# Folding w_phi into the key weights with two row tiles of 64 rows

## The chip, the cores and the metric

The kernel runs on one core of one Trainium2 chip. The metric is the device time of one execution in microseconds (us); lower is better. A core has five engines that run their own instruction streams: TensorE (PE; its weight loads are shown apart as PEld), VectorE (DVE), ScalarE (ACT), GpSimd (POOL) and SyncE (SP), which here issues the DMAs. Matrix products go from SBUF to PSUM, from which ScalarE or VectorE reads them.

## The reference

Two identical layers are applied to x (2048 tokens, D = 640). Each layer has a linear attention and a dense part; the attention has 32 heads of 20 columns:

```python
qkv = layernorm(x) @ wqkv                        # q, k, v, per head 20 columns
pq, pk = q @ w_phi, k @ w_phi                    # per head, 20 x 20
phi = concat(softmax(p), softmax(-p))            # 40 features per head
kv, z = phi_k^T v, sum(phi_k)
x = x + (phi_q kv / (phi_q z + 1e-6)) @ wo
x = x + mish(layernorm(x) @ w1 + b1) @ w2
```

## The kernel before

**Folding.** A softmax does not change when one number is taken from all its inputs, so the kernel subtracts the last of the 20 columns of each head from the other 19 and keeps 19 columns per head. It multiplies w_phi, shifted in this way, into the query and key weights once, at the start of the first layer. The result is a matrix of 640 rows (five chunks k of 128) and 32 x 19 = 608 columns. It is kept in two parts, a rounded high part (`r1h`, written by ScalarE out of PSUM) and the rest (`r1l`, written by VectorE as PSUM minus the high part); every later product uses high times high, high times low and low times high.

`load_raw` fetches the transposed query or key weights in six tiles (`raw`), 120 rows (six heads) each for the first four and 80 rows (four heads) for the last two. `bd` holds w_phi as block diagonals of 120 x 120, `shift_phi` does the subtraction on GpSimd. `fold_part` (L258) multiplies one `raw` tile, 128 columns of it at a time as the stationary operand, with one block of `bd`. For a chunk, three such products fill 18 heads (342 columns) in one PSUM bank and three more the other 14 heads (266 columns) in another, and `fold_end` (L286) evicts each bank by one ScalarE and one VectorE instruction. `fold_phi` (L290) does this for the keys in two visits within the first block of tokens: four half chunks in two `mm` tiles (two PSUM banks each), and later six half chunks in two `mm` tiles and two `one` tiles (a bank each). There are two `mm` buffers and four `one` buffers, which all projections share.

**Projections and features.** The 2048 tokens are worked through in eight blocks of two tiles of 128. `project` computes a tile of keys, queries or values by 30 matmuls (L414). `features` makes the softmax pairs: copy out of PSUM on ScalarE, maximum and minimum on VectorE (L439), two subtractions (L440 and L442), the exponential on ScalarE, sums and reciprocals on VectorE (L448, L449), and the scaling on GpSimd (L450). Subtraction L440 is on GpSimd for queries and on VectorE for keys, as the argument `pool_sub` says. Then query features are transposed on VectorE (L505) and written to DRAM (`e_d`), and key features are multiplied with the values into `kva` (L491). In the second half of the layer `average` (L768) uses column halves: outputs of 64 partitions, each with its own stationary operand of 64 columns.

**Order.** The start of the first layer stands in a `written()` block, in which instructions stay in the order of the text. Behind it a planner orders the instructions of each engine by simulated times; `tc.issue_after` keeps an instruction behind another one. Within an engine the order is fixed when the program is built. The DMAs of SP are spread over eight completion counters in turn, and each waits until the DMA eight places earlier has landed. In the first block the order of the work is q0, v0, first visit of the fold, v1, second visit, k0, q1, k1; the statistics of block 1 (L307, L309, L319) and its normalization (`xn`, L135) lie in between on VectorE, GpSimd and ScalarE.

Of the kernel before, what the change touches and what calls it, by code (L numbers as in the profile page):

```python
# [8 lines left out]
F32 = mybir.dt.float32  # L9
# [7 lines left out]
P = 128  # L17
# [27 lines left out]
def kernel(  # L45
# [22 lines left out]
    def mm_tile():  # L68
        return psum.tile([P, 2, 512], F32, tag="mm", name="mm", bufs=2)

    def one_tile():
        return psum.tile([P, 512], F32, tag="one", name="one", bufs=4)
# [169 lines left out]
    def load_raw(which, ts=range(6)):  # L242

        raw = []
        for t in ts:
            rows = 120 if t < 4 else 80
            if t < 5:
                r = wts.tile([P, D], F32, tag=f"r2{'hl'[which]}{5 + t}", name=f"raw{which}{t}")
            else:
                r = r2_wide(10 + which, F32)[:, 0]  # L250

            n = P if t < 5 else rows
            c0 = which * D + (t * 120 if t < 5 else D - rows)
            nc.sync.dma_start(r[:n], wqk_t[c0:c0 + n, :])
            raw.append((r, rows))
        return raw

    def fold_part(ps, k, t, bd, raw):  # L258

        r, rows = raw[t]  # L260
        heads = rows // DH
        n = DL * (6 * (t % 3) if t < 5 else 10)
        ins = nc.tensor.matmul(ps[:, n:n + heads * DL].rearrange("p (j d) -> p j d", d=DL), r[:rows, k * P:(k + 1) * P],
                         bd[:rows, t, :rows].rearrange("p (j d) -> p j d", d=DH)[:, :, :DL], start=True, stop=True)
        last_product[0] = ins.ins
# [20 lines left out]
    def fold_end(ws, ps, k, c):  # L286
        fold_high(ws, ps, k, c)
        fold_low(ws, ps, k, c)

    def fold_phi(ws, bd, raw, parts):  # L290

        for n in range(0, len(parts), 2):
            mm = mm_tile() if n < 4 else None
            pair = list(zip(parts[n:n + 2], [one_tile(), one_tile()] if mm is None else [mm[:, 0], mm[:, 1]]))
            with tc.issue_after(last_product[0]):
                for (k, c), ps in pair:
                    for t in range(3 * c, 3 * c + 3):
                        fold_part(ps, k, t, bd, raw)
            for (k, c), ps in pair:
                fold_end(ws, ps, k, c)  # L300


    def norm_stats(t, xt):

# [155 lines left out]
    def attend_first(layer, x_src, first):  # L460
# [18 lines left out]

        def keys(xts, i, v):  # L480
            e = big_tile()
            yield from features(project(xts, i % BT, kv_ws, 0, w=QC), e, False,
                                nc.vector if i == NT - 1 else nc.gpsimd)
            yield
            if i % BT == 0 and BT < i < NT - BT:
                yield
            for r in range(9):
                for j in range(4):
                    h = 3 * (4 * (r // 3) + j) + r % 3
                    if h < H:  # L490
                        nc.tensor.matmul(kva[32 * j:32 * j + DH + 1, 40 * r:40 * r + 40],  # L491
                                         v[:, (DH + 1) * h:(DH + 1) * (h + 1)], e[:, 40 * h:40 * h + 40],
                                         start=(i == 0 and r == 0), stop=(i == NT - 1), skip_group_check=True)
# [32 lines left out]
        if first is None:  # L526
            with written():
                xt = fetch(x_src, 0)
                bd = big_tile()[:120, :720].rearrange("p (t c) -> p t c", t=6)
                nc.sync.dma_start(bd[:, :3], phi_bd[:, :3])  # L530
                raw_q = load_raw(0, range(3))

                nc.vector.memset(bd[:80, 5, :80], 0.0)
                nc.sync.dma_start(bd[:40, 5, :40], phi_bd[80:120, 4, 80:120])
                nc.sync.dma_start(bd[40:80, 5, 40:80], phi_bd[:40, 5, :40])
                nc.sync.dma_start(bd[:, 3:5], phi_bd[:, 3:5])
                shift_phi(bd, slice(0, 3))
                raw_q += load_raw(0, range(3, 6))
                kv_ws = [r1_pair(k) for k in range(KD)]
                raw_v = [fetch_v(k) for k in range(KD)]  # L540
                raw = load_raw(1)
                early = fetch(x_src, 1)
                mvs = [norm_stats(t, xt) for t in range(BT)]
                norm_scale(0, mvs)
                shift_phi(bd, slice(3, 5))
                shift_phi(bd, 5)

                q_ws = [r2_pair(k) for k in range(KD)]
                mm = [mm_tile(), mm_tile()]
                pcs = [one_tile(), mm[0][:, 0], mm[0][:, 1], mm[1][:, 0], mm[1][:, 1]]  # L550
                for t in range(3):
                    for k in range(KD):
                        fold_part(pcs[k], k, t, bd, raw_q)
                xn = [row_tile() for _ in range(BT)]
                act(xn[0], xt[:, 0, :], AF.Identity, bias=stats[:, 0, 1, 0:1], scale=stats[:, 0, 0, 0:1])
                nc.vector.tensor_scalar(xn[1], xt[:, 1, :], stats[:, 0, 0, 1:2], stats[:, 0, 1, 1:2],
                                        op0=ALU.mult, op1=ALU.add)

                def highs(c, ks):
                    for k in ks:  # L560
                        fold_high(q_ws, pcs[k], k, c)

                def lows(c, ks):
                    for k in ks:
                        fold_low(q_ws, pcs[k], k, c)

                def make_v(k, low):
                    split(kv_ws[k][0][:, D:2 * D], kv_ws[k][1][:, D:2 * D], raw_v[k], low)

                def half(c, ks):  # L570
                    project_half(q0[c], nxt, 0, q_ws, 0, c, ks, w=QC)

                highs(0, (0, 1, 2))
                lows(0, (0,))
                nxt = Transposed(xn)
                nxt.turn(one_tile())
                nxt.high()
                lows(0, (1, 2))
                nxt.lower()
                highs(0, (3, 4))  # L580
                pcs[0], pcs[1] = one_tile(), one_tile()
                for k in (0, 1):
                    fold_part(pcs[k], k, 3, bd, raw_q)
                nxt.turn(one_tile())
                for t in (4, 5):
                    for k in (0, 1):
                        fold_part(pcs[k], k, t, bd, raw_q)
                last = mm_tile()
                nxt.turn(last[:, 0])
                nxt.high()  # L590
                nxt.high()
                lows(0, (3, 4))
                nxt.lower()
                nxt.lower()
                highs(1, (0, 1))
                q0 = [one_tile()]
                half(0, (0, 1))
                mm = mm_tile()
                pcs[2], pcs[3] = mm[:, 0], mm[:, 1]
                for k in (2, 3):  # L600
                    for t in range(3, 6):
                        fold_part(pcs[k], k, t, bd, raw_q)
                lows(1, (0, 1))
                half(0, (2, 3))
                make_v(0, nc.gpsimd)
                highs(1, (2, 3))
                lows(1, (2, 3))
                pcs[4] = last[:, 1]
                for t in range(3, 6):
                    fold_part(pcs[4], 4, t, bd, raw_q)  # L610
                half(0, (4,))
                make_v(1, nc.gpsimd)
                highs(1, (4,))
                lows(1, (4,))
                q0.append(one_tile())
                half(1, range(KD))
                for k in (2, 3, 4):
                    make_v(k, nc.vector)
            nc.sync.dma_start(mask, bass.AP(tensor=head_mask.tensor, offset=head_mask.offset,
                                            ap=[[1, 120], [120 * (DH + 1), 3]]))  # L620
        else:
            nxt, kv_ws, turn = first
            with tc.issue_after(last_load[0]):
                load_k_weights(kv_ws)
            q_ws = load_q_weights()
        for b in range(NB):
# [15 lines left out]
            for n, (kind, t) in enumerate(order):  # L642
                t = int(t)
                i = b * BT + t
                if b == 0 and layer == 0 and n in (2, 3):
                    if n == 2:
                        advance()
                    fold_phi(kv_ws, bd, raw, ((0, 0), (1, 0), (2, 0), (3, 0)) if n == 2 else
                             ((4, 0), (0, 1), (1, 1), (2, 1), (3, 1), (4, 1)))
                if b == 0 and n == (1 if layer else 3):  # L650
                    kva = one_tile()
                    nc.vector.memset(kva[:, :360], 0.0)
# [464 lines left out]
```

## Time and profile before

| what | value |
|---|---|
| median of 3 runs | 1357.27 us (1356.24 to 1361.53) |
| the profiled execution | 1357.15 us, its span 1355.4 us |
| PE busy | 1347.9 us, 99% |
| VectorE, ScalarE, GpSimd busy | 78%, 42%, 34% |
| share of PE in the chain that ended last | 94% |

The span is the time from the first to the last instruction. A row of a timeline is: start in us, duration in us (of a merged group from its first start to its last end), engine, line, operation, what it writes `<-` what it reads, shapes, count; in brackets the idle time of the engine before it and what ended that. `raw` and `bd` appear as `raw` and `big` (the buffer that holds `bd`). A row of a table of windows is: the stretch, its length, then for PE, PEld, DVE, ACT and POOL the busy time and number of instructions, the granted TensorE clock, the share of the DMA engines and the rate in GB/s. A row of the chain is: start, duration, engine or DMA, tile, line and count. One f32 matmul is two records of the trace.

### The profile page before, as it was taken

To read this page: it belongs to the slowest core of one execution; us is meant where nothing else is said; L and a number is where in the kernel's file an instruction comes from. 1 tells how busy PE (TensorE), PEld (TensorE's weight loads), DVE (VectorE), ACT (ScalarE), POOL (GpSimd) and SP (SyncE) were. 2 spreads that over 40 slices of the span, in tenths; PEclk is the share of its full clock that TensorE was granted. 3 is DMA by queue.
4 is the path that set the end of the run, shared out by engine and by line. 5 is a ranking of instruction groups with operands and counts; after the bars stand their busy time and mean duration, and the time that the engine had idled before them with its cause. 6 is when DMAs were issued, how large, how long until landed. Compare 5 with 4: busy or idle time off the path is not lost.

```text
span 1355.4 us, 30982 instructions
## 1 busy us (share of the span) xinstructions
PE 1347.9 (99%) x12896; PEld 1337.4 (99%) x12896; DVE 1061.2 (78%) x1799; ACT 575.7 (42%) x968; POOL 462.4 (34%) x417
## 2 busy tenths in 40 slices
PE   9999999999999999999999999999999999999999
PEld 9999999999999999999999999999999999999998
DVE  6888988886787887778769788788768776676775
ACT  5444444212454545445443334332236444444443
POOL 3355544334222222222225655634251211111112
PEclk9999999999999999999999999999999999999999
DMA  9544444698714442244474534548974221233200
GB/s 332 166 101 92 95 111 99 173 289 280 216 35 95 117 118 71 61 104 104 140 231 100 122 79 90 95 102 263 282 259 127 79 68 41 88 98 98 70 29 20
DMA packets 352629, 174.11 MB, mean 128 GB/s; under 512 B 287449, under 2 KB 324041, under 8 KB 352489
## 3 DMA queue, kind: packets, MB, share of 16 engines
q1 hardware_dynamic: 352489, 172.14, 46.9%
q8 instruction: 101, 1.65, 0.5%
q14 instruction: 39, 0.32, 0.1%
HBM read 106.23 MB, written 65.86 MB: 127 GB/s over the span
## 4 chain that ended last, share of the span: by engine, by line
PE 94%; DVE 2%; DMA 2%; POOL 1%; SPq 1%; ACT 0%; issue 0%; POOLq 0%; ACTq 0%
PE mm L414 26%; PE one L892 25%; PE mm L943 24%; PE one L414 12%; PE mm L768 2%; PE one L334 2%; PE one L491 1%; PE one L943 1%; DMA xt<-in_x 1%; PE one L768 1%; DVE r L448 1%; DMA raw<-in_wqk_t 0%; DVE m L439 0%; DMA v<-in_wv 0%; DVE r L442 0%; SPq L508 0%
## 5 line engine op out<-in xcount | busy, mean ns | idle before, releaser
L943 PE MATMUL mm<-r2h,ol 128*128 128x320 f32 x1240 | 296.1, 309 | 0.0
L918 POOL TENSOR_TENSOR ol<-big,ol 128x512 fp32r<-128x512 f32 (+1 forms) x98 | 131.1, 1338 | 477.7 <-ACT ol L917 419.5
L892 PE MATMUL one<-xtl,r1h 128*128 128x256 f32 x960 | 268.2, 279 | 0.0
L892 PE MATMUL one<-xth,r1l 128*128 128x256 f32 x960 | 268.0, 279 | 0.0
L892 PE MATMUL one<-xth,r1h 128*128 128x256 f32 x960 | 265.9, 279 | 0.0
L943 PEld LDWEIGHTS mm<-r2h,ol 128*128 128x128 f32 x1240 | 212.5, 188 | 0.0
L943 PE MATMUL mm<-r2l,ol 128*128 128x320 f32 x620 | 191.2, 309 | 0.0
L414 PE MATMUL mm<-r1h,xth 128*128 128x304 f32 (+1 forms) x600 | 185.2, 309 | 0.0
L414 PE MATMUL mm<-r1l,xth 128*128 128x304 f32 (+1 forms) x600 | 183.7, 306 | 0.0
L414 PE MATMUL mm<-r1h,xtl 128*128 128x304 f32 (+1 forms) x600 | 183.6, 306 | 0.2 <-POOL xtl L351 0.2
L892 PEld LDWEIGHTS one<-xtl,r1h 128*128 128x128 f32 x960 | 180.4, 188 | 0.0
L892 PEld LDWEIGHTS one<-xth,r1l 128*128 128x128 f32 x960 | 180.4, 188 | 0.0
L892 PEld LDWEIGHTS one<-xth,r1h 128*128 128x128 f32 x960 | 179.6, 188 | 0.0
L907 DVE TENSOR_SCALAR big<-big 128x512 f32<-128x512 f32 (+1 forms) x98 | 57.2, 583 | 110.0 <-ACT big L905 109.8
L909 ACT ACTIVATE big<-big,two 128x512 f32<-128x512 f32 (+1 forms) x98 | 70.1, 715 | 116.1 <-DVE big L908 116.1
L917 ACT ACTIVATE ol<-big 128x512 fp32r<-128x512 f32 (+1 forms) x98 | 60.9, 622 | 137.6 <-DVE big L916 137.4
L905 ACT ACTIVATE big<-one,b1s 128x256 f32<-128x256 f32 x192 | 80.9, 468 | 89.0 <-PE one L892 88.5
L450 POOL TENSOR_TENSOR r<-r,r 128x1280 f32<-128x1280 f32 x32 | 77.2, 2413 | 118.9 <-DVE r L449 100.8
L943 PEld LDWEIGHTS mm<-r2l,ol 128*128 128x128 f32 x620 | 116.4, 188 | 0.0
L414 PEld LDWEIGHTS mm<-r1h,xth 128*128 128x128 f32 x600 | 112.8, 188 | 0.9
L414 PEld LDWEIGHTS mm<-r1h,xtl 128*128 128x128 f32 x600 | 112.8, 188 | 0.4 <-POOL xtl L351 0.4
L414 PEld LDWEIGHTS mm<-r1l,xth 128*128 128x128 f32 x600 | 112.8, 188 | 0.1
(161 smaller groups left out, 3142.7 us busy)
## 6 DMA issues: line engine op xcount, KB each, us to landing
e_d<-r SPq DMA_DIRECT2D x128, 160.0 KB, 4.2
big<-e_d SPq DMA_DIRECT2D x32, 640.0 KB, 8.0
x_d<-xt SPq DMA_DIRECT2D x23, 640.0 KB, 4.8
xt<-x_d SPq DMA_DIRECT2D x22, 640.0 KB, 5.3
n_d<-xn SPq DMA_DIRECT2D x168, 80.0 KB, 2.3
xt<-in_x SPq DMA_DIRECT2D x16, 640.0 KB, 4.4
xn<-x_d SPq DMA_DIRECT2D x28, 320.0 KB, 4.4
v<-n_d SPq DMA_DIRECT2D x30, 256.0 KB, 3.0
```

The lines of the kernel that those rows point to most:

```text
L334: nc.tensor.transpose(ps[:, c, t * P:(t + 1) * P], self.rows[t][:, (c0 + c) * P:(c0 + c + 1) * P], ident)
L414: last_product[0] = nc.tensor.matmul(ps[:, :w], a[:, sl], r, start=(k == 0 and n == 0), stop=(k == KD - 1 and n == 2)).ins
L448: nc.vector.tensor_reduce(r, eg, axis=AX.X, op=ALU.add)
L450: ins = scale.tensor_tensor(eg, eg, r.unsqueeze(2).to_broadcast([P, 2 * H, DH]), op=ALU.mult).ins
L768: nc.tensor.matmul(po[c][64 * q:64 * q + 64, GW * j:GW * j + w], phs[g][:n, s0:s0 + 64], kvb[:n, g, :w], start=True, stop=True)
L892: nc.tensor.matmul(ph[:, j, :], l, r, start=(n == 0), stop=(n == 3 * KD - 1))
L905: exps[0] = nc.scalar.activation(part(ta, 0)[:, j - js.start], ph[:, j, :], AF.Exp, bias=b1s[:, 2 * pr + j:2 * pr + j + 1]).ins
L907: nc.vector.tensor_scalar_min(e, e, E_CAP)
L909: nc.scalar.activation(r, n, AF.Ln, bias=two)
L917: nc.scalar.activation(ah[:, js], n, AF.Copy)
L918: nc.gpsimd.tensor_tensor(al[:, js], n, ah[:, js].bitcast(F32), op=ALU.subtract)
L943: ins = nc.tensor.matmul(pys[t][c][:, :HC], (ah, ah, al)[n][:, j, t * P:(t + 1) * P], w, start=(f == 0 and n == 0), stop=(f == KF - 1 and ...
```

## The change

The key weights are folded by another arrangement; the query weights are folded as before.

- `load_phi_halves` builds `ph`, a second copy of w_phi: 64 rows for the first three heads of a `raw` tile and 60 rows for the other three, each with blocks of 60 columns. It is cleared on VectorE, filled by three DMAs ahead of those of the key `raw` tiles, and shifted by one more `shift_phi` on GpSimd.
- The key `raw` tiles are loaded four rows earlier, so that one head triple lies in rows 4 to 63 and the other in rows 64 to 123. The sixth tile has 64 rows instead of 80, of which the last 40 (two heads) count.
- `fold_keys` replaces `fold_phi`. For a chunk it issues 11 matmuls: for each of five `raw` tiles one per row half (three heads, 57 columns), and one for the last two heads (38 columns). The row halves write to two PSUM banks. Chunks 0 to 3 take an `mm` tile each, chunk 4 two `one` tiles. The first visit does chunks 0 and 1, the second chunks 2, 3 and 4.
- A chunk in an `mm` tile is evicted by one pair of instructions for 570 columns of both banks and one for the last 38; chunk 4 by pairs for 285, 285 and 38 columns.
- In the first layer the keys of the first four tiles have subtraction L440 on GpSimd.

```diff
-            n = P if t < 5 else rows
-            c0 = which * D + (t * 120 if t < 5 else D - rows)
+            if which:
+                n = P if t < 5 else 64
+                c0 = D + (120 * t - 4 if t < 5 else D - n)
...
-    def fold_phi(ws, bd, raw, parts):
...
+    def load_phi_halves():
+
+        ph = pair_tile(F32).rearrange("p a s -> p (a s)")[:, :360].rearrange("p (t c) -> p t c", t=6)
+        nc.vector.memset(ph, 0.0)
+        for s in range(2):
+            nc.sync.dma_start(ph[4 + 60 * s:64 + 60 * s, :5], phi_bd[60 * s:60 * s + 60, :5, 60 * s:60 * s + 60])
+        nc.sync.dma_start(ph[24:64, 5, :40], phi_bd[:40, 5, :40])
+        return ph
+
+    def fold_keys(ws, ph, raw, ks):
+
+        w = 3 * DL
+        for k in ks:
+            mm = mm_tile() if k < KD - 1 else None
+            ps = [one_tile(), one_tile()] if mm is None else [mm[:, 0], mm[:, 1]]
+            with tc.issue_after(last_product[0]):
+                for t in range(6):
+                    heads = 3 if t < 5 else 2
+                    for s in range(2 if t < 5 else 1):
+                        rows = slice(64 * s, 64 + 60 * s)
+                        last_product[0] = nc.tensor.matmul(
+                            ps[s][:, t * w:t * w + heads * DL].rearrange("p (j d) -> p j d", d=DL),
+                            raw[t][0][rows, k * P:(k + 1) * P],
+                            ph[rows, t, :heads * DH].rearrange("p (j d) -> p j d", d=DH)[:, :, :DL],
+                            start=True, stop=True).ins
+            pairs = [x[:, :10 * w].rearrange("p (t s d) -> p s t d", s=2, d=w) for x in ws[k]]
+            ends = [x[:, 10 * w:QK] for x in ws[k]]
+            if mm is None:
+                outs = [(ps[s][:, :5 * w].rearrange("p (t d) -> p t d", d=w), *(x[:, s] for x in pairs))
+                        for s in range(2)]
+            else:
+                outs = [(mm[:, :, :5 * w].rearrange("p s (t d) -> p s t d", d=w), *pairs)]
+            for src, hi, lo in outs + [(ps[0][:, 5 * w:5 * w + 2 * DL], *ends)]:
+                nc.scalar.activation(hi, src, AF.Copy)
+                last_fold[0] = nc.vector.tensor_tensor(lo, src, hi.bitcast(F32), op=ALU.subtract).ins
...
-            yield from features(project(xts, i % BT, kv_ws, 0, w=QC), e, False,
+            yield from features(project(xts, i % BT, kv_ws, 0, w=QC), e, not layer and i < 2 * BT,
...
                 raw_v = [fetch_v(k) for k in range(KD)]
+                ph = load_phi_halves()
                 raw = load_raw(1)
...
                 for k in (2, 3, 4):
                     make_v(k, nc.vector)
+                shift_phi(ph, slice(0, 6))
...
-                    fold_phi(kv_ws, bd, raw, ((0, 0), (1, 0), (2, 0), (3, 0)) if n == 2 else
-                             ((4, 0), (0, 1), (1, 1), (2, 1), (3, 1), (4, 1)))
+                    fold_keys(kv_ws, ph, raw, (0, 1) if n == 2 else (2, 3, 4))
```

In the changed kernel's line numbers the matmuls of `fold_keys` are L314 and its evictions L327 (ScalarE) and L328 (VectorE).

More of the change, by code (lines that the diff above doesn't have):

```diff
@@ L250, in load_raw @@
                 r = r2_wide(10 + which, F32)[:, 0]
-            n = P if t < 5 else rows
-            c0 = which * D + (t * 120 if t < 5 else D - rows)
+            if which:
+                n = P if t < 5 else 64
+                c0 = D + (120 * t - 4 if t < 5 else D - n)
+            else:
+                n = P if t < 5 else rows
+                c0 = t * 120 if t < 5 else D - rows
             nc.sync.dma_start(r[:n], wqk_t[c0:c0 + n, :])
@@ L288, in fold_end @@
         fold_low(ws, ps, k, c)
-    def fold_phi(ws, bd, raw, parts):
-        for n in range(0, len(parts), 2):
-            mm = mm_tile() if n < 4 else None
-            pair = list(zip(parts[n:n + 2], [one_tile(), one_tile()] if mm is None else [mm[:, 0], mm[:, 1]]))
-            with tc.issue_after(last_product[0]):
[L296 to L300, printed above, removed]
+    def load_phi_halves():
[5 more added lines that the diff above has]
+        return ph
@@ new lines, in fold_keys @@
+    def fold_keys(ws, ph, raw, ks):
[3 more added lines that the diff above has]
+            ps = [one_tile(), one_tile()] if mm is None else [mm[:, 0], mm[:, 1]]
+            with tc.issue_after(last_product[0]):
+                for t in range(6):
[12 more added lines that the diff above has]
+                        for s in range(2)]
+            else:
+                outs = [(mm[:, :, :5 * w].rearrange("p s (t d) -> p s t d", d=w), *pairs)]
+            for src, hi, lo in outs + [(ps[0][:, 5 * w:5 * w + 2 * DL], *ends)]:
+                nc.scalar.activation(hi, src, AF.Copy)
+                last_fold[0] = nc.vector.tensor_tensor(lo, src, hi.bitcast(F32), op=ALU.subtract).ins
```

## The prediction

> **What bounds the kernel now.** I read the page first (busy times), then the chain that ended last over the first 75 us, a table of windows there, and each engine's timeline around the folding.
>
> ```profile
> span 1355.4 us, 30982 instructions
> PE 1347.9 (99%) x12896; PEld 1337.4 (99%) x12896; DVE 1061.2 (78%) x1799; ACT 575.7 (42%) x968; POOL 462.4 (34%) x417
> ```
> ```profile
> 24.20:27.00 2.80, 2.80 (x27) 2.80 (x26) 2.60 (x8) 2.25 (x4) 0.56 (x3) 1.00 1.04 403
> 45.00:60.00 15.00, 15.00 (x110) 15.00 (x109) 13.50 (x19) 6.26 (x8) 3.65 (x2) 1.00 0.41 144
> ```
> ```profile
> 15.95 8.43 DMA xt<-in_x
> 24.41 1.67 DVE bn L307 x4
> ...
> 30.09 1.72 ACT xn L135 x2
> ...
> 62.52 0.76 PE one L491 x64
> ```
>
> PE is busy 99%, at a granted clock of 1.00 (the figure before the DMA share in the windows). Only two things can therefore move the end: PE work added or removed, and PE made to wait. The order in the built program differs from before only in roughly the first 75 us; behind that PE runs the same instructions. So the forecast is the shift of PE at about 45 us, where it is busy 15.00 of 15.00. The chain shows what already presses there: VectorE's statistics (L307) wait until 24.38 (15.95 + 8.43) for block 1 of x. The profiled execution took 1357.15 us (span 1355.4 and 1.75 around it), 0.12 below the median of 1357.27; the sum is made against 1357.15.
>
> **PE work of the fold.**
>
> ```profile
> 24.12 0.31 PE L414 MATMUL one<-r1h,xtl 128*128 128x320 f32 x1
> 24.27 2.83 PE L263 MATMUL mm<-big,raw 120*128 120x114 f32 x24
> 26.87 0.39 PE L414 MATMUL one<-r1h,xth 128*128 128x320 f32 x1
> 27.10 0.31 PE L414 MATMUL one<-r1l,xth 128*128 128x320 f32 x1
> ...
> 31.38 1.31 PE L263 MATMUL mm<-big,raw 120*128 120x114 f32 x10
> ...
> 33.29 0.64 PE L263 MATMUL mm<-big,raw 120*128 120x114 f32 x4 [0.38 <-DVE r1l L283]
> ...
> 34.66 0.61 PE L263 MATMUL one<-big,raw 120*128 120x114 f32 x4
> 35.11 0.39 PE L263 MATMUL one<-big,r 80*128 80x76 f32 x2
> 35.33 0.61 PE L263 MATMUL one<-big,raw 120*128 120x114 f32 x4
> ...
> 36.00 1.13 PE L334 MATMUL one<-ident,xn 128*128 128x128 f32 x8
> ```
>
> One f32 matmul is two records. 24 records run from 24.27 to 26.87, 0.108 each; six records, four of them 76 columns wide, from 34.66 to 35.33, 0.112 each. The pitch, 0.111, follows neither the moving columns (114 or 76) nor the rows (120 or 80); what they share is a stationary operand of 128 columns. The 30 matmuls removed are 60 x 0.111 = 6.66 us. The 55 added (five chunks of 11) are 110 records, also of 128 stationary columns. Upper bound: one after the other, 110 x 0.111 = 12.2, that is +5.55. If the two row halves run side by side, a chunk is five pairs and the lone matmul of the last two heads: 6 x 2 x 0.111 = 1.33, five chunks 6.66, that is 0. Lower bound: side by side, and half the rows also halve the load: 3.33, that is -3.33; 80 against 120 rows show nothing of the kind. The nearest rows for halves are those of L768, which splits the array by columns:
>
> ```profile
> 267.58 0.31 PE L414 MATMUL one<-r2h,xtl 128*128 128x320 f32 x1
> 267.82 1.39 PE L768 MATMUL mm<-kvb,big 120*64 120x63 f32 x40
> 269.04 0.27 PE L768 MATMUL mm<-kvb,ol 80*64 80x42 f32 x4
> 269.12 1.36 PE L768 MATMUL mm<-kvb,big 120*64 120x63 f32 x40
> ...
> 272.88 0.27 PE L768 MATMUL mm<-kvb,ol 80*64 80x42 f32 x4
> 273.08 0.42 PE L414 MATMUL one<-r2h,xth 128*128 128x320 f32 x1
> 273.34 0.31 PE L414 MATMUL one<-r2l,xth 128*128 128x320 f32 x1
> ```
>
> 44 records take 1.30 (267.82 to 269.12), 0.030 each; 64 columns in sequence would take half of 0.111, 0.055. The column halves overlap, so I take overlap for row halves too: 0.
>
> The Trainium skill ("TensorE: Matmul & The Clock Gate", LDWEIGHTS) says that a weight load takes as long as its columns, whatever its rows. The 80- and 120-row records agree, so by this rule the halves save nothing on PE. Its "TensorEngine Tiling (Array Packing)", Key Properties, says that a change of tiling mode drains TensorE; the rows of L768 agree with some 0.3 us per visit, worked out next.
>
> **Going in and out of halves.** Into L768 0.24 (267.58 to 267.82) instead of 0.15: 0.09. Out of it: 272.88 + 4 x 0.030 = 273.00 to 273.08, 0.08, then 0.26 instead of 0.15 for the first matmul, 0.11. A visit is about 0.28. Full-height folding pays 0.08 (26.87 to 27.10, 0.23). So +0.2 for each of two visits.
>
> **Loads.** Three DMAs for ph (two of 60 x 5 x 240 bytes = 72 KB, one of 6.4 KB) go onto SP's queue ahead of the raw key rows, of block 1 and of block 2.
>
> ```profile
> GB/s 0 0 0 0 0 0 0 0 0 0 0 0 0 20 138 141 140 126 159 138 139 128 131 109 147 131 150 167 156 152 147 144 133 112 70 104 4 0 0 0
> ```
>
> While these loads run the DMA engines are full (share 1.04 and 403 GB/s in the first window above). The fence is the DMA rate in 40 equal slices from 66 to 75 us, where e_d moves in rows of 128 bytes: about 140 GB/s. 150 KB cost between 0.39 (at 390) and 1.07 (at 140); the last raw tile loses 16 rows of 2.5 KB, -0.1. I take +0.6 (ends +0.3 and +1.0) for block 1's landing: 24.98. The raw rows have cover: block 1's 640 KB needs 1.6 us at 390 GB/s, so the tile ahead of it had landed by about 22.8, then 23.4; PE's first matmul of ph comes at 24.27, the one on the last tile 1.1 later. Without that cover each 0.1 of lateness is 0.1 on PE.
>
> **The release of the PSUM tiles.** Each chunk now fills a mm tile (there are two) and is read four times: ScalarE 570 columns, VectorE 570, ScalarE 38, VectorE 38, each waiting for the other engine. Chunk 3 reuses chunk 1's tile, and in VectorE's order chunk 1's 38-column read stands behind the transpose of the first query tile (L505), which waits for GpSimd's scaling (L450), which waits for the reciprocal (L449).
>
> ```profile
> 28.02 1.27 DVE L307 BATCH_NORM_STATS2 bn<-xt 128x6 f32<-128x320 f32 x3
> 29.20 0.50 DVE L283 TENSOR_TENSOR r1l<-mm,r1h 128x342 fp32r<-128x342 f32 x1
> 29.62 0.22 DVE L319 SCALAR_TENSOR_TENSOR stats<-mv,stats 128x1 f32<-128x1 f32 x2
> ...
> 30.18 0.54 DVE L449 RECIPROCAL r<-r 128x64 f32<-128x64 f32 x1
> ...
> 32.63 0.52 DVE L283 TENSOR_TENSOR r1l<-mm,r1h 128x342 fp32r<-128x342 f32 x1 [1.40 <-ACT r1h L279]
> 33.26 1.51 DVE L505 STREAM_TRANSPOSE r<-r 128x1280 f32<-128x1280 f32 x1
> ...
> 44.94 0.81 DVE L440 TENSOR_TENSOR big<-big,m 128x640 f32<-128x640 f32 x1
> ```
> ```profile
> 21.90 1.27 POOL L440 TENSOR_TENSOR r<-r,m 128x640 f32<-128x640 f32 x1 [0.59 <-DVE m L439]
> ...
> 30.86 2.36 POOL L450 TENSOR_TENSOR r<-r,r 128x1280 f32<-128x1280 f32 x1 [3.34 <-DVE mv L309]
> ...
> 55.70 2.37 POOL L450 TENSOR_TENSOR big<-big,r 128x1280 f32<-128x1280 f32 x1 [6.99 <-DVE r L449]
> ```
>
> 342 columns take 0.50 and 640 take 0.81, so 570 take about 0.73 and 38 about 0.19. With 0.6 for block 1, the statistics end at 29.9 instead of 29.3; L319 to 30.1; 570 columns of chunk 0 to 30.85; reciprocal to 31.3; GpSimd 31.5 to 33.9; transpose to 35.4; 38 columns to 35.6; PE starts chunk 3 at 35.75 (0.13 later, as 33.15 to 33.29 before). Before, the second tile of this visit started at 33.29. So +2.46. Of this PE waits in two pieces: chunk 2 for chunk 0's 38 columns, which ScalarE reads behind its two xn (1.72 from about 30.5), so until about 32.8 instead of 31.6, 1.2 us; then 1.33 of work, and chunk 3 from 34.1 to 35.75, 1.6 us. The waits swallow the switch of the first visit. From there to the transposes of xn PE needs two chunks, 2.66, instead of 2.71 (33.29 to 36.00): -0.05. Out of halves: +0.2. The second transposition takes a PSUM tile of chunk 4, read last by VectorE behind a lower half of x of 512 columns (about 0.68 by the same line); most of that lies beside the 15 matmuls in between, and I estimate +0.2.
>
> **What is hidden.** Ten ScalarE evictions become eleven of nearly the same columns, off the path but for the chain above. VectorE's clearing of ph stands ahead of the statistics for which it waits until the first x lands; GpSimd's shift of ph (about as long as an L440 of 640 elements, 1.27) has 24.27 as its limit and starts near 19. Four subtractions leave VectorE (0.81 each) for GpSimd (1.27): it is busy 3.65 of 15 us there, and the first keys' scaling ends at 58.07 against PE's use at 62.52, 4.4 of cover. VectorE's second subtraction (L442) waits behind each; without cover a tile costs 0.46 and a handover of some 0.6.
>
> **Sum:** 2.46 - 0.05 + 0.2 + 0.2 = +2.8; 1357.15 + 2.8 = 1360.0.
>
> **The rivals.**
> 1. The row halves run in sequence. For it: no row halves in this trace. Against: L768. First visit 22 matmuls x 0.222 = 4.88 instead of 2.60, second 33 x 0.222 = 7.33 instead of 4.62 (31.38 to 36.00), 0.2 twice, 0.1: +5.5, 1362.6. Chunk 3's turn then comes at 36.4 (24.27 + 4.88 + 0.3 + 4.51 + 2.44), after its release: no wait.
> 2. No new wait: the small reads are not what PE waits for, and the 0.38 of before vanishes while the two visits' 0.4 stays. For it: a tile may be given back as soon as its 570 columns are read. Against: the four reads of one tile and VectorE's order. 1357.15 - 0.38 + 0.4 = 1357.2.
> 3. Slower: halves in sequence, and each change of half also shows part of its load, as the change of line at 26.87 does (0.08). 55 x 0.08 = 4.4 on rival 1: +9.9, 1367.0. From 0.024 per change it passes 6.8 us. Against: the halves of L768 change as often at 0.030.
> 4. Half the rows load in half the time. The wait stays, and behind it two chunks take 1.33 less: +1.5, 1358.6. The Trainium skill ("TensorEngine Tiling (Array Packing)", Theoretical Speedup) allows up to 2x for short contractions; nothing here shows that for loads.
>
> **How the numbers follow.** Chances: forecast 0.60 (1358.6 to 1361.2, from the ends of the load and the small estimates), rival 1 0.18, rival 2 0.10, rival 3 0.06, rival 4 0.06. The range takes in all but rival 3, with 0.6 and 0.8 beyond rivals 2 and 1 for their switches and the loads: 1356.6 to 1363.4. 0.5% is 6.8 us, about what a measurement can tell here; only rival 3 passes it: slower 0.07, faster 0.02, same 0.91.
>
> **What the changed profile would show.** L314's records: 22 per chunk in about 1.33 us (right), 2.4 (rival 1), 0.7 (rival 4). PE waits of about 1.2 us ahead of chunk 2 and 1.6 us ahead of chunk 3, the latter released by VectorE's 38-column L328 right behind L505; none means rival 2. Block 1 landing near 25.0. PE full from 45 us on, L491 not waiting for GpSimd. The prediction fails if PE waits again behind 45 us, for GpSimd's later scaling above all.

## The result and the profile after

| | before | after |
|---|---|---|
| median | 1356.68 us (1355.89 to 1361.53, 7 runs) | 1363.40 us (1362.96 to 1368.84, 7 runs) |
| the profiled execution | 1357.15 us, span 1355.4 | 1364.34 us, span 1362.6 |

The ratio is 1.0053 with a 95% interval of 1.0035 to 1.0070. The kernel became slower by about 7 us; the prediction had said +2.8 and a time of 1360.0, with "same" at 0.91. The measured median lies at the upper edge of the predicted range, and the profiled executions differ by 7.19 us.

The page of the changed kernel first: its busy times, and the granted TensorE clock in 40 slices of 34 us.

```profile
span 1362.6 us, 31092 instructions
PE 1352.6 (99%) x12946; PEld 1341.5 (98%) x12946; DVE 1064.3 (78%) x1797; ACT 576.1 (42%) x969; POOL 467.8 (34%) x422
PEclk9899999999999999999999999999999999999999
```

PE's idle time did grow, but only by 2.5 us (span minus busy time: 7.5 before, 10.0 after). The other 4.7 us are PE *busy* for longer, although the records added in the fold fit side by side. The clock row shows an 8 in the second slice, 34 to 68 us; in the profile before, that row is all 9. The windows of the changed kernel, and below them those of the kernel before in the same place, show where it lies:

```profile
24.17:26.80 2.63, 2.63 (x45) 2.63 (x44) 1.44 (x4) 2.28 (x4) 0.00 (x0) 1.00 1.01 395
31.50:36.00 4.50, 1.64 (x23) 1.43 (x23) 3.05 (x9) 2.96 (x9) 3.44 (x4) 0.98 1.05 347
36.00:46.00 10.00, 9.99 (x64) 9.90 (x65) 5.60 (x15) 2.54 (x7) 0.53 (x4) 0.50 0.91 248
46.00:53.00 7.00, 7.00 (x53) 7.00 (x52) 3.20 (x6) 1.19 (x3) 2.08 (x3) 0.99 0.88 291
```
```profile
31.40:36.00 4.60, 4.22 (x37) 4.10 (x37) 3.18 (x8) 2.84 (x9) 2.90 (x4) 1.00 0.82 286
36.00:46.00 10.00, 10.00 (x76) 9.90 (x75) 7.03 (x19) 2.88 (x7) 1.39 (x6) 1.00 0.93 263
```

From 36 to 46 us PE is busy 9.99 of 10 us at a granted clock of 0.50. The busy share alone would call this a full engine; only the clock column, and the fewer instructions in it, show the loss. The stretch at half clock is 10.24 us long (35.8 to 46.1), so it costs at most half of that, 5.1 us. The timeline of PE in the changed kernel shows the two waits and the same instructions at both clocks:

```profile
24.17 1.33 PE L314 MATMUL mm<-ol,raw 64*128 64x57 f32 x20
...
25.49 1.34 PE L314 MATMUL mm<-ol,raw 60*128 60x57 f32 x19
...
32.90 1.33 PE L314 MATMUL mm<-ol,raw 64*128 64x57 f32 x20 [1.26 <-DVE r1l L328]
...
36.01 2.38 PE L314 MATMUL mm<-ol,raw 64*128 64x57 f32 x20 [1.62 <-DVE stats L346]
...
45.20 0.46 PE L441 MATMUL mm<-r1h,xth 128*128 128x304 f32 x1
...
46.48 0.30 PE L441 MATMUL mm<-r1h,xth 128*128 128x304 f32 x1
```

Twenty records of a chunk take 1.33 us in the first visit and 2.38 at half clock; a product of 304 columns takes 0.46 instead of 0.30.

The chain that ended last, in the changed kernel and then in the kernel before, gives the account in two pieces:

```profile
18.31 7.27 DMA xt<-in_x
25.58 0.02 issue
25.61 1.67 DVE bn L334 x4
...
30.61 0.66 DVE r1l L328
31.28 0.46 DVE r L476
31.73 0.15 DVE mv L336 x2
31.88 2.37 POOL r L477
34.25 0.02 issue
34.27 0.04 DVE r L532
34.31 1.40 issue
35.71 0.16 DVE r1l L328
...
36.01 2.54 PE mm L314 x21
...
53.16 16.78 PE mm L441 x120
```
```profile
33.29 1.53 PE mm L263 x12
...
45.74 16.78 PE mm L414 x120
```

The second tile of the second visit starts at 36.01 instead of 33.29: +2.72. The same stretch of 120 projection matmuls starts at 53.16 instead of 45.74: +7.42, so another +4.70 came between those points, which is where the clock is halved. The spans differ by 7.2.

### The profile page after: what moved, and what is told of

Same layout as the page of the kernel before. It is cut to its first block, busy times and chain, and to the rows that moved or that the text cites. A ratio compares the mean times of both kernels' runs of the same rounds, so it can differ in the third digit from the quotient of the medians.

```text
span 1362.6 us, 31092 instructions
## 1 busy us (share of the span) xinstructions
PE 1352.6 (99%) x12946; PEld 1341.5 (98%) x12946; DVE 1064.3 (78%) x1797; ACT 576.1 (42%) x969; POOL 467.8 (34%) x422
## 4 chain that ended last, share of the span: by engine, by line
PE 91%; DVE 4%; DMA 2%; SPq 1%; POOL 1%; issue 1%; ACT 0%; ACTq 0%; POOLq 0%
PE one L920 25%; PE mm L441 24%; PE mm L971 24%; PE one L441 11%; PE one L361 2%; PE mm L796 2%; PE one L518 1%; DMA e_d<-r 1%; DVE r L475 1%; PE one L971 1%; SPq L535 1%; DVE m L466 1%; PE one L796 1%; DMA xt<-in_x 1%; DMA big<-in_wv 1%
## 5 line engine op out<-in xcount | busy, mean ns | idle before, releaser
L477 POOL TENSOR_TENSOR r<-r,r 128x1280 f32<-128x1280 f32 x32 | 76.6, 2395 | 118.0 <-DVE r L476 109.8
```

The costliest lines, as they stand in the source:

```text
L477: ins = scale.tensor_tensor(eg, eg, r.unsqueeze(2).to_broadcast([P, 2 * H, DH]), op=ALU.mult).ins
```

## The experiments

Each is an edit of one of the two kernels, and each diff is against the kernel that the text names. Times are medians, each ratio is against runs of the kernel before on the same chip, and the brackets are 95% intervals. PE waits are those at the matmuls of the fold. "At half clock" is the length of the stretch at or behind the fold whose granted clock is 0.50 in the profiled execution; the half clock at the very end of the program, where the work runs out, is not counted.

| label | edit | PE waits, us | at half clock, us | ratio |
|---|---|---|---|---|
| (the change) | | 1.26, 1.62 | 10.24 | 1.0053 [1.0035, 1.0070] |
| e9_fold_only | without GpSimd's subtractions | 1.62, 1.62 | 10.24 | 1.0062 [1.0046, 1.0079] |
| e10_sub_only | GpSimd's subtractions alone | 0.7 in two | none | 1.0005 [0.9996, 1.0015] |
| e1_highs_first | evictions of a chunk regrouped | 0.56, 1.06 | 6.8 (and 3.4 at 922 us) | 1.0038 [1.0023, 1.0053] |
| e2_filled | waits filled with extra products | 0.28 | 6.8 | 1.0045 [1.0029, 1.0061] |
| e5_filled_wide | the same, products twice as wide | 0.45 | none | 1.0030 [1.0018, 1.0041] |
| e3_two_waits | before, two waits added | 1.80, 0.76 | 6.8 | 1.0034 [1.0022, 1.0045] |
| e4_one_wait | before, one wait meant to be added | 0.80, 2.41 | 6.8 | 1.0038 [1.0025, 1.0052] |
| e6_narrow_full_height | before, each product in two halves of its columns | none | 10.2 | 1.0093 [1.0078, 1.0108] |
| e11_wide_with_waits | the change, products twice as wide | 1.86 | none | 1.0026 [1.0015, 1.0036] |
| e7_early_x | e1, block 1 loaded earlier | 0.84 | 6.8 | 1.0025 [1.0014, 1.0036] |
| e8_early_x_wide | e7, products twice as wide | 0.71, behind the fold | none | 1.0018 [1.0009, 1.0028] |
| e12_before_early_x | before, block 1 loaded earlier | 0.7 in two | none | 1.0000 [0.9992, 1.0009] |

**Which part of the change it is.** First the two edits one at a time. The fold alone, from the changed kernel:

```diff
-            ... features(project(xts, i % BT, kv_ws, 0, w=QC), e, not layer and i < 2 * BT,
+            ... features(project(xts, i % BT, kv_ws, 0, w=QC), e, False,
```

> The changed kernel with its GpSimd part undone: the keys of the first four tiles have subtraction L440 on VectorE again. All of the loss is put down to the second visit of the fold, so this should change nothing: the two waits of 1.3 and 1.6 us, the clock at 0.50 behind them, ratio 1.005. A rival in which GpSimd's four subtractions cost something: ratio below 1.004.

The subtractions alone, from the kernel before:

```diff
-            ... features(project(xts, i % BT, kv_ws, 0, w=QC), e, False,
+            ... features(project(xts, i % BT, kv_ws, 0, w=QC), e, not layer and i < 2 * BT,
```

> The kernel before with the GpSimd part alone: four subtractions of 0.81 us move from VectorE to GpSimd, where they take 1.27. PE does not wait for either there, so nothing: clock 1.00, ratio 1.000, within 0.001. The rival: above 1.001.

The fold carries the whole loss (1365.19 us alone), and its half-clock stretch is that of the full change:

```profile
35.90:46.00 10.10, 10.10 (x66) 10.00 (x66) 5.58 (x15) 2.54 (x7) 0.43 (x3) 0.50 0.91 247
```

Four subtractions on GpSimd cost nothing that can be measured (1356.88 against 1356.88).

**Is it the waits, or the row halves?** Two theories stood at the start: I, the waits (TensorE idle) bring the clock down; H, the row halves do it themselves. `e1_highs_first` shortens the waits: all ScalarE evictions of a chunk first, then all VectorE subtractions, so that the tile no longer goes back and forth.

```diff
-            for src, hi, lo in outs + [(ps[0][:, 5 * w:5 * w + 2 * DL], *ends)]:
+            outs.append((ps[0][:, 5 * w:5 * w + 2 * DL], *ends))
+            for src, hi, lo in outs:
                 nc.scalar.activation(hi, src, AF.Copy)
+            for src, hi, lo in outs:
                 last_fold[0] = nc.vector.tensor_tensor(lo, src, hi.bitcast(F32), op=ALU.subtract).ins
```

> The changed kernel, with all ScalarE evictions of a chunk ahead of its VectorE ones, so that the 38-column reads no longer stand behind the xn and behind the transpose L505. Two theories of why PE's granted clock fell to 0.50 from 36.0 to 46.1 us in the changed kernel. Theory I (idle): PE stood idle for 1.26 and 1.62 us within 4.4 us. Theory H (halves): matmuls of 60 rows and 57 columns count as too little work. Here the first wait should go and the second shrink to about 1.1 us, while the row halves stay. Theory I: the clock stays at 1.00, the sum is 34.05 - 33.29 + 0.2, about +1.0 on before, ratio 1.0007. Theory H: the clock still falls to 0.50 for some 10 us, ratio about 1.0045.

The waits shrank from 2.9 us in all to 1.6, so the alternation of the two engines on one PSUM tile was a real part of them. But the clock still fell, for 6.8 us instead of 10.24 (window and waits of this run):

```profile
35.35:42.10 6.75, 6.75 (x49) 6.67 (x48) 4.81 (x13) 2.22 (x6) 0.89 (x2) 0.50 1.05 292
```
```profile
PE mm L314 <- DVE r1l L330: 1.6, 2, 1.1
```

The first wait was expected to go and did not quite. Far behind the fold the clock of this execution fell once more, to 0.50 from 922.8 to 926.2 us, behind a PE wait of 1.98 us for ScalarE (L135). That is not at the fold. It costs at most 1.7 us; this execution, at 1364.02 us, lies 3.0 above the median.

`e2_filled` keeps TensorE occupied instead. Nine matmuls of the value projection ahead of the second visit and the 11 matmuls of chunk 2 are issued twice; what the first ones write is overwritten.

```diff
-                for t in range(6):
+                for t in (*range(6), *range(6)) if k == 2 else range(6):
...
-                pv = project(xts, i, kv_ws, D, [one_tile(), one_tile()])
+                pv = [one_tile(), one_tile()]
+                if i == 1:
+                    project_half(pv[1], xts, i, kv_ws, D, 1, range(3), last=2)
+                project(xts, i, kv_ws, D, pv)
```

> The changed kernel, with PE work put into its two waits: nine matmuls of v1's projection issued twice (1.32 us, ahead of the second visit) and chunk 2's 11 folding matmuls issued twice (1.33 us). Results are the same; nothing is left out. The evictions and their order stay, so chunk 3 should still start near 36.0. Theory I (idle): what is left of the waits is under 0.4 us, the clock stays at 1.00, and the time is the one forecast for the changed kernel, +2.9 on before, ratio 1.0021. Theory H (halves): more matmuls of halves do not help, the clock falls as in the changed kernel, ratio 1.0053.

One wait of 0.28 us was left, and the clock still fell, for 6.8 us:

```profile
32.20:36.60 4.40, 4.05 (x66) 3.99 (x67) 3.23 (x6) 1.75 (x5) 2.50 (x4) 1.00 0.96 318
36.60:43.40 6.80, 6.80 (x43) 6.72 (x41) 4.34 (x12) 2.54 (x7) 0.00 (x0) 0.50 0.92 206
```

In the 4.4 us ahead of it PE was busy 4.05, nearly as much as in the kernel before at that place (4.22 of 4.60), where nothing happens. Theory I in its plain form fell. `e3_two_waits` and `e4_one_wait` go the other way: the old fold at full height, with waits made by repeating VectorE's reads of a tile (`e4_one_wait` has only the entry `(3, 0): 2`).

```diff
-        fold_low(ws, ps, k, c)
+        for _ in range({(1, 0): 4, (3, 0): 2}.get((k, c), 1)):
+            fold_low(ws, ps, k, c)
```

> The kernel before, full-height folding, with VectorE evictions repeated (chunk 1's first half four times, chunk 3's twice), which holds back the two mm tiles of the second visit: PE waits of about 1.3 and 1.2 us with 1.3 us of work between. No row halves anywhere. Theory I (idle): 2.5 us of idle in 3.8 us is nearly what the changed kernel has (2.9 in 4.3), the clock falls to 0.50 for some 8 to 10 us, +1.9 for the waits and +4 to +5 for the clock, ratio about 1.0047. Theory H (halves): the clock stays at 1.00, +1.9, ratio 1.0014.

> The kernel before, with chunk 3's VectorE eviction of the first visit issued twice: one PE wait of about 2.4 us instead of two, the same 2.4 or so of idle time in one piece. Theory I (idle) with a window of a few us: the clock falls as with two waits, ratio about 1.0047; if the clock should need either more than 2.4 us of idle time or two waits, 1.00 and 1.0014. Theory H (halves): 1.00 and ratio 1.0014.

```profile
31.06:35.40 4.34, 1.78 (x14) 1.70 (x15) 4.24 (x10) 2.15 (x6) 3.08 (x4) 1.00 0.83 309
35.40:42.20 6.80, 6.80 (x34) 6.80 (x34) 3.68 (x10) 2.55 (x6) 0.00 (x0) 0.50 0.85 176
```
```profile
37.20:44.00 6.80, 6.80 (x31) 6.80 (x31) 4.00 (x11) 2.07 (x5) 1.24 (x6) 0.50 0.92 237
```

The clock fell in both (first fence e3, second e4), without a row half anywhere. `e4_one_wait` did not make one wait, as expected, but two, of 0.80 and 2.41. So waits suffice, and so does what `e2_filled` has with next to no wait. H fell as the only cause as well.

**What the two have in common.** In the fold TensorE spends its time loading weights: the pitch is 0.111 us whether 114 or 57 columns follow. The rows of L768 bound how long columns stream: a half of the array passes 63 columns within 0.060 us (two halves side by side at 0.030), so 57 take at most 0.054, half of the pitch, and 114 at most 0.109, nearly all of it. (The 0.43 and 0.86 that the expectations use lie within these bounds; no run measures them.) So theory S: what counts is the share of time, over a few us, in which columns stream through the array; waits and narrow products lower it alike. Its rival R: the rows in use. `e5_filled_wide` is `e2_filled` with every product of a row half writing its 57 columns twice, side by side (the second copy lands on columns that a later product or nobody uses): same loads, same rows, twice the columns.

```diff
-                            ps[s][:, t * w:t * w + heads * DL].rearrange("p (j d) -> p j d", d=DL),
+                            ps[s][:, t * w:t * w + 2 * heads * DL].rearrange("p (r j d) -> p r j d", r=2, d=DL),
...
-                            ph[rows, t, ...][:, :, :DL],
+                            ph[rows, t, ...][:, :, :DL].unsqueeze(1).to_broadcast([60 if s else 64, 2, heads, DL]),
```

> The filled kernel again (row halves, next to no wait), but each matmul of a half streams its columns twice: 114 (or 76) instead of 57 (or 38), the second copy into PSUM columns that the next matmul overwrites or nobody reads. Nothing is left out. The filled kernel's clock fell although PE hardly waited, and the full-height kernels with waits fell too, so neither idle time nor row halves alone explains it. Theory S (streaming): what counts is the share of time in which columns are streamed. A record's pitch is 0.111 us by its weight load, and 114 columns fill about 0.86 of it, 57 columns 0.43. Theory R (rows): what counts is how many rows of the array work. Theory S: the same pitch, the clock stays at 1.00, about +2.9 on before, ratio 1.002. Theory R: the clock falls as before widening, ratio 1.0045.

`e6_narrow_full_height` is the opposite test, from the kernel before: each product of 120 or 80 rows is split into two of half the columns, at full height, with no halves and no waits.

```diff
+    def fold_narrow(ps, k, t, bd, raw):
+        r, rows = raw[t]
+        heads = rows // DH // 2
+        n = DL * (6 * (t % 3) if t < 5 else 10)
+        for s in range(2):
+            last_product[0] = nc.tensor.matmul(
+                ps[:, n + s * heads * DL:n + (s + 1) * heads * DL].rearrange("p (j d) -> p j d", d=DL),
+                r[:rows, k * P:(k + 1) * P],
+                bd[:rows, t, s * heads * DH:(s + 1) * heads * DH].rearrange("p (j d) -> p j d", d=DH)[:, :, :DL],
+                start=True, stop=True).ins
...
-                        fold_part(ps, k, t, bd, raw)
+                        fold_narrow(ps, k, t, bd, raw)
```

> The kernel before, with every matmul of the key fold split into two of half the columns (57 or 38), 120 or 80 rows high: 60 matmuls instead of 30, no row halves, each with its own weight load, so 60 x 0.222 = 13.3 us instead of 6.7, +6.7. PE has little to wait for as it comes later. Theory S (streaming): 0.43 of the time streamed, the clock falls to 0.50 within or behind the fold, for multiples of 3.3 us, and then the fold is slower still: +10 to +13, ratio 1.0075 to 1.0095. Theory R (rows): 1.00 throughout, +6.7, ratio 1.005.

The windows of `e5_filled_wide`, at the place where `e2_filled` fell, and then of `e6_narrow_full_height`:

```profile
32.20:36.60 4.40, 3.96 (x67) 3.91 (x67) 2.77 (x8) 1.66 (x6) 2.94 (x4) 1.00 0.97 256
36.60:43.40 6.80, 6.80 (x66) 6.72 (x64) 5.01 (x14) 2.24 (x7) 0.16 (x1) 1.00 0.90 270
```
```profile
24.20:29.60 5.40, 5.40 (x51) 5.40 (x49) 5.39 (x15) 2.77 (x5) 1.08 (x3) 1.00 1.04 404
34.00:38.20 4.20, 4.20 (x40) 4.20 (x39) 1.21 (x5) 1.22 (x3) 0.00 (x0) 1.00 0.70 136
38.20:48.40 10.20, 10.20 (x49) 10.20 (x49) 4.39 (x11) 2.23 (x6) 0.38 (x3) 0.50 0.96 297
```

In `e5_filled_wide` the clock stayed at 1.00, in the profile and in each of its 8 runs, with PE idle a little more than in `e2_filled` (3.96 against 4.05 busy) and the same rows. What differs is the columns, and the place of the one wait. In `e6_narrow_full_height` the clock fell for 10.2 us behind a stretch in which PE was busy 4.20 of 4.20. Both go with S and against R and I. One row seems not to: the first visit there (24.2 to 29.6) is narrow for 5.4 us too, and nothing fell.

The traces allow a closer reading, made after the runs and not forecast. In each profiled execution the changes of the clock are whole steps of 3.41 us apart: the stretches at half clock last one, two or three such steps (3.41, 6.83, 10.24 us). So count, for one step, the columns of the matmul records that start in it; halves that run side by side count half (the column quarters of L491 a quarter).

| kernel | step, us | PE busy, us | columns | clock in the next step |
|---|---|---|---|---|
| the change | 32.42 to 35.83 | 1.50 | 608 | 0.50 |
| e4_one_wait | 33.74 to 37.15 | 1.51 | 1178 | 0.50 |
| e2_filled | 33.20 to 36.61 | 3.13 | 1368 | 0.50 |
| e6_narrow_full_height, second visit | 34.80 to 38.21 | 3.41 | 1406 | 0.50 |
| e3_two_waits | 32.02 to 35.43 | 1.81 | 1444 | 0.50 |
| e6_narrow_full_height, first visit | 24.56 to 27.97 | 3.41 | 1710 | 1.00 |
| e4_one_wait, one step earlier | 30.32 to 33.74 | 2.11 | 1856 | 1.00 |
| e11_wide_with_waits | 32.72 to 36.13 | 2.96 | 2831 | 1.00 |
| e5_filled_wide | 32.38 to 35.79 | 3.07 | 2888 | 1.00 |
| before | 33.68 to 37.09 | 3.41 | 3076 | 1.00 |

The columns put the steps in order; PE's busy time does not. It holds in all 14 profiled executions: the nine falls before the end of the program come behind steps of 608 to 1444 columns, and no step behind which the clock stayed at 1.00 has fewer than 1518. At the end of the program, where the work runs out, `e10_sub_only` has a fall behind a step with 1920, so the limit is not sharp to some 400 columns. Three things stay open. Columns weighted by the rows in use separate the steps as well (falls up to 1327, none from 1447 on, apart from that same last step), so rows alone are excluded, but streaming is not told apart from multiply-adds. What share of the time the limit is, these runs do not show, since none measures how long a column of the fold takes. And records can be missing from a trace.

**The changed kernel with its clock kept up.** `e11_wide_with_waits` applies the widening alone to the changed kernel.

> The changed kernel, each matmul of a half streaming its columns twice (114 or 76), nothing else changed: the two waits stay, the folding streams 0.86 of the time instead of 0.43. Theory S (streaming) counts a wait as time without streaming: 2.9 us of waits in 4.3 us still make the clock fall, but folding behind them no longer holds it down, so half clock for about 6.7 us instead of 10: +2.7 and +3.3, ratio 1.0044. If narrow halves alone had done it and waits did not matter: clock 1.00, ratio 1.002.

The planner moved things, and one wait of 1.86 us took the place of the two, which was not expected. Chunks 2 to 4 then run without a break, at full clock, as does all behind them:

```profile
31.30:33.17 1.87, 0.01 (x2) 0.03 (x1) 1.65 (x6) 1.87 (x7) 1.02 (x1) 1.00 1.00 352
33.17:37.30 4.13, 4.13 (x66) 4.06 (x66) 2.82 (x6) 1.03 (x4) 2.42 (x4) 1.00 0.85 207
37.30:47.00 9.70, 9.70 (x70) 9.41 (x70) 4.55 (x13) 3.39 (x9) 0.54 (x3) 1.00 0.90 241
```

A wait longer than either of the changed kernel's left the clock alone here, with wide products around it. The widening is not the only difference, though: PE waits 1.86 us in all instead of 2.88, and most of the wait lies in the step of 3.41 us ahead of the one in the table, which still has 3840 columns. `e1_highs_first` is the nearer neighbour: 1.62 us of waits, narrow products, and a fall. The time, 1359.93 us (1.0026), is close to the predicted 1.0021, but with one wait where the prediction had two. The difference to the changed kernel is 0.0027 of 1357, or 3.7 us; the intervals of the two ratios are too wide to compare it closely with the 4.7 us read off the trace.

**Can the change be repaired?** `e7_early_x` is `e1_highs_first` with block 1's load issued ahead of the key rows, to remove the rest of the waits; `e8_early_x_wide` adds the widening; `e12_before_early_x` does the early load in the kernel before.

```diff
+                early = fetch(x_src, 1)
                 ph = load_phi_halves()
                 raw = load_raw(1)
-                early = fetch(x_src, 1)
```

> The changed kernel, with ScalarE's evictions of a chunk first and block 1 of x loaded ahead of ph and the raw key rows, so that statistics and xn come about a microsecond earlier. The two waits should shrink to about 0.3 in all; the row halves of 57 columns stay. Theories S and R alike: the clock still falls for some 3.4 or 6.7 us (half of that is lost), about +0.3 for the waits and halves and +3.3: ratio 1.0027. If idle time mattered after all, 1.00 and ratio 1.000.

> As the run with block 1 loaded early, and each half streams its columns twice, as in the widened one. Theory S (streaming): the clock stays at 1.00 and the fold costs what it did before: -0.4 for the wait of before, +0.4 for going in and out of halves, +0.3 for what is left of the waits, ratio 1.0002, and the version that comes nearest to the kernel before. Theory R (rows): as without widening, ratio 1.0027.

> The kernel before, with block 1 of x loaded ahead of the raw key rows and nothing else changed: the statistics come earlier, and the one PE wait in the second visit (0.38 us in the profile of before) should go. The version that could beat both kernels, by 0.4 us at most: ratio 0.9997, not to be told from 1.000; if the later raw key rows hold up PE in the first visit instead, up to +1 us, ratio 1.0007. The clock stays at 1.00 either way.

The early load left a wait of 0.84 us in `e7_early_x`, and the clock fell in the profiled execution (0.51 from 34.8 to 41.7); the mean clocks of its other runs go from 0.996 to 1.000, and its times from 1356.88 to 1362.20, so there the fall is decided anew in each execution. With wide products (`e8_early_x_wide`) the mean clock was 1.000 or 0.999 in every run, the fold had no wait left, and the time is 1.0018 instead of the expected 1.0002; 0.71 us of that is a new wait of the projection behind the fold, and the rest is not explained. The early load is worth nothing to the kernel before: where that has one wait of 0.38 us in the second visit, `e12_before_early_x` has two, of 0.30 and 0.38. No version here beats the kernel before.

## Why the prediction was wrong

The step that failed is the sentence on which the sum was built: PE is busy "at a granted clock of 1.00 [...]. Only two things can therefore move the end: PE work added or removed, and PE made to wait". The clock was taken as given, and it was a third thing, at nothing in the sum: behind the start of the second tile at 36.01 us, where the sum had +0.35 (-0.05 + 0.2 + 0.2), the trace has +4.70, and the clock is 0.50 there for 10.24 us. No rival had it, although the trace of before holds a price for it. Its first matmuls are 30 transposes (L92):

```profile
1.34 5.93 PE L92 MATMUL one<-ident 128*128 128x128 f32 x30 [1.34 <-POOL ident masks.py:199]
```

Their records start 0.213 us apart up to 6.3 us and 0.109 us apart from there on, which is also the pitch of the later transposes of that shape (L334). The granted clock reads 1.00 there too, so only the pitch shows that TensorE can run at half speed. The range's upper end, 1363.4, was set by rival 1, which did not happen; that the measured median of 1363.40 lies on it is chance.

- *The row halves run side by side* was right: 22 records of a chunk from 24.17 to 25.49, 1.32 us against 1.33 predicted. Rivals 1, 3 and 4 fell with that, and with rival 4 the gain that the Trainium skill ("TensorEngine Tiling (Array Packing)", Theoretical Speedup) allows for short contractions: the halves buy no time where the weight load sets the pitch. What they do is make each product half as wide, which no term of the sum priced.
- *The release of the PSUM tiles* was right nearly to the tenth: waits of 1.26 and 1.62 against 1.2 and 1.6, the same chain of L328, L476, L477, L532 and the 38-column L328. The trace names L346 as the releaser of the second, which comes right behind that L328. Rival 2 (no wait) fell. `e1_highs_first` shows the alternation of the two engines at work. The shift at that point was +2.72 against +2.46.
- *The loads* were mis-sized: block 1 landed at 25.58 (18.31 + 7.27) instead of 24.38, +1.20, where +0.6 was taken and +1.0 was the outer end. The chain starts there, so this alone would have moved the release by 0.6 more than forecast; the steps behind it took some 0.3 less than estimated, which left 2.72 against 2.46.
- *The switches out of halves and the second transposition*, +0.2 each, are too small to be told apart behind a halved clock. *Hidden* was right: GpSimd's four subtractions are free in `e10_sub_only`, and PE is full from 46 us on (7.00 of 7.00).

Why the clock fell is shown in part. That waits alone do it (`e3_two_waits`, `e4_one_wait`), that narrow products alone do it (`e6_narrow_full_height`, and `e2_filled` with 0.28 us of wait), and that wider products at the same pitch prevent it (`e5_filled_wide` with 0.45 us of wait, and, with less waiting than in the changed kernel, `e11_wide_with_waits`): these are measured. That the quantity behind all three is how much streams through the array in a step of 3.41 us is the simplest reading of them, and the count above bears it out, but no profile has a column for it. Whether it is columns or multiply-adds, and the exact limit, are open. The count also accounts for the length of the fall: the changed kernel's first two steps at half clock have 864 and 1471 columns and the third 3728, behind which the clock is back; in `e1_highs_first` the second has 2706 and already suffices.

The Trainium skill ("TensorE: Matmul & The Clock Gate", What's actually happening) has two clock states and a free-running window of 3413 ns. The trace agrees with the states, 1.00 and 0.50, and the stretches of 3.4, 6.8 and 10.2 us are one, two and three such windows. Its rule of thumb (Why this matters for your kernels), no idle gaps above some 3 us, is not enough here: the longest gap was 1.62 us in the changed kernel, and there was none in `e6_narrow_full_height`.

## What to carry to other kernels

Read the granted clock of each stretch beside the busy share before calling an engine full, and ask of every edit that adds waits or narrows products how many columns the array still streams in each few us: a second clock state can cost more than the waits that bring it (here 4.7 us against 2.9). Where weight loads set the pitch, splitting a product into row halves of half the width saves nothing on TensorE, even though the halves overlap (a chunk takes 1.32 us here). A PSUM tile that two engines read in turn is held through every handover; reading it with one engine to the end and then with the other cut the waits from 2.9 to 1.6 us in `e1_highs_first`.

## What the hardware showed that was not expected

- TensorE's clock can fall to 0.50 while PE counts as busy all the time (4.20 of 4.20 ahead of the fall, 10.20 of 10.20 during it).
- It changes in steps of 3.41 us: at the fold it stays down for two (6.8 us, five kernels) or three (10.2 us, three kernels), and for one late in `e1_highs_first` (3.4 us). The loss is at most half of that: 1.7, 3.4 or 5.1 us.
- What the falls have in common is few columns in the step ahead, 608 to 1444 of the some 7600 that a step of wide projections can hold, and not an idle PE.
- At the same pitch, 114 columns a product keep the clock up where 57 do not.
- Whether it falls can differ between executions of one kernel (`e7_early_x`: mean clocks of 0.996 to 1.000).
